# Order of VectorE's and ScalarE's work in the attention periods of a sigmoid-attention and MLP kernel

## The chip, the cores and the metric

The kernel runs on one core of one Trainium2 chip. The metric is the device time of one execution in microseconds (us); of several runs the median counts. Engines are named as in the profile: PE (TensorE) multiplies matrices and writes PSUM, PEld is its weight load, DVE is VectorE, ACT is ScalarE, POOL is GpSimd, SP is SyncE, on whose queue all DMAs are issued.

## What is computed

```python
scores = (q @ k.transpose(0, 1, 3, 2)) / sqrt(64) - log(448)     # 8 batches, 12 heads, 448 rows, 64 columns
attn   = sigmoid(scores)
x      = (attn @ v).transpose(0, 2, 1, 3).reshape(3584, 768)
out    = square(maximum(x @ w_in, 0)) @ w_out                      # 768 -> 2048 -> 768
```

`q`, `k`, `v` are 32-bit floats; `w_in` and `w_out` come as 64-bit floats, and the kernel makes 32-bit ones of them itself, from the two 32-bit words of each number.

## The kernel before

**The attention** works on pairs of heads: 48 pairs, two in each of 24 periods, numbered d = 0 to 23. `block(d)` (line 435) writes out by hand, for every engine, the order of the work of period d; nothing reorders it later. With n = 2d, TensorE computes in a period first `sr` (line 288), the rows left over of both pairs, then three score tiles of 128 rows for pair n and three for pair n+1 (`sc`, line 272), and then `pav`, the product with v, of pair n and of pair n+1 (lines 303 and 315). Score matmuls run in three passes on a split of x (here q and k of a pair): `high` (line 494, `qh`) casts x to a rounded part on VectorE, `low` (line 498, `ql`) subtracts that from x; the passes are high by high, high by low, low by high. ScalarE applies the sigmoid to each tile (`at` and `rest`, line 260).

Score tiles and `pav` share four PSUM tiles in rotation (`two`, line 537). A period takes nine of them, in the order `sr`, three `sc`, three `sc`, two `pav`; so the second score tile of a period takes the place of `pav` of pair n-2, and the third that of pair n-1. Each `pav` comes in two halves. `take(n)` (line 321) copies one half to SBUF on ScalarE, `put(n)` (line 325) adds the other half to it on VectorE: these are the *sums of x* (`xo`), the attention's output.

**The weights' words** are converted beside the attention. Chunks of 768 numbers a row (`f`) are loaded by `weights_load`, two operations of ScalarE treat the upper words (line 148) and the lower ones (line 149), and a *join* puts them together: three operations of VectorE (lines 153, 154, 157) and an integer add of GpSimd (line 160). Of two joined chunks VectorE makes four sums of blocks (lines 169 to 172), and chunk and sums are stored. `weights_of(piece, n)` spreads these steps over the pairs. In a period the *first* place for a join or for the four weight sums is ahead of `put(n-2)`, the *second* is ahead of the last `low`.

**The MLP** computes each product of 2x2 blocks by seven products of sums of blocks. The sums of x for its first group are *pieces* (`x_operands`, line 343): pieces 1, 2, 3, 6 split blocks of x into a high part (three casts on ScalarE, line 332) and a low part (three subtractions on VectorE, line 336, put off to the next period's list `later`); `t1`, `t2`, `t3` are three subtractions each (line 361) in place. `PIECES` and `T_PIECES` (lines 67 and 68) name the periods in which they are made. The MLP's weights are split in the same way by `halve_weights` (line 233): a cast on ScalarE (line 237) and a subtraction on VectorE (line 238). After the attention come, four times, a first product (`gemm1`, `ha`, `hb`, `hc`, line 547) and a second (`gemm2`, `oa`, `ob`, `oc`).

**SBUF tiles** come from pools of equal slots (`op2` with 35, `op1` with 20, `wide` with 8); a load whose slot isn't free waits on SP, and what is queued on SP behind it waits too. Before period 0, eight matmuls on zeros (line 765) keep TensorE at work while the first loads run.

Of the kernel before, what the change touches and what calls it, by code (L numbers as in the profile page):

```python
# [63 lines left out]
DEFERRED = (5, 6, 7)  # L64


PIECES = {12: (1,), 14: (2,), 20: (3,), 22: (6,)}
T_PIECES = {22: ("t1", "t2"), 23: ("t3",)}


@with_exitstack
def sigmoid_attention_relu2_mlp(
# [46 lines left out]
    nc = tc.nc  # L119
# [24 lines left out]

    def convert_words(t, w):
        nc.scalar.activation(w, t[:, :, 1], AF.Abs)
        nc.scalar.mul(out=t.bitcast(I32)[:, :, 0], in_=t.bitcast(U32)[:, :, 0], mul=2.0**-29)

    def convert_join(t, w):
# [29 lines left out]
    def deferred(i, at):  # L181


        f, a, s = {}, {}, {}

        def load(n, u, k):
            t = op2(f"fd{n}_{i}").rearrange("p a s -> p (a s)")[:, : 2 * HALF]
            nc.sync.dma_start(out=t.bitcast(I32), in_=w_out[u][:, k * HALF : (k + 1) * HALF].bitcast(I32))
            f[n] = t.rearrange("p (n w) -> p n w", w=2)

        def block(n):
            return op1(f"b{n}_{i}")[:, :HALF]

        def words(n):
            a[n] = block(n)
            convert_words(f[n], a[n])

        def add_up():
            for n in (5, 6, 7, 3):
                s[n] = block(n)  # L200
            nc.vector.tensor_add(out=s[5], in0=a[0], in1=a[4])
            nc.vector.tensor_sub(out=s[6], in0=s[5], in1=a[1])
            nc.vector.tensor_sub(out=s[7], in0=a[1], in1=a[0])
            nc.vector.tensor_sub(out=s[3], in0=a[2], in1=s[6])

        def store():
            for n, t in (a | s).items():
                if n:
                    nc.sync.dma_start(out=w2[i][:, PLACE[1][n]], in_=t)

        out = []
        for b, (n, u, k) in enumerate(((1, i, 0), (0, i, 1), (4, i + NI, 0), (2, i + NI, 1))):
            out.append((at + 3 * b - 5, lambda n=n, u=u, k=k: load(n, u, k)))
            out.append((at + 3 * b, lambda n=n: words(n)))
            out.append((at + 3 * b + 1, lambda n=n: convert_join(f[n], a[n])))
        out.append((at + 12, add_up))
        out.append((at + 13, store))
        return out
# [11 lines left out]
    def load_w1(i, parts, name):  # L230
        return load_weights([w1[i][:, part] for part in parts], name)

    def halve_weights(w):

        hi, lo = w
        raw = lo.bitcast(F32)
        nc.scalar.copy(out=hi, in_=raw)  # L237
        nc.vector.tensor_sub(out=lo, in0=raw, in1=hi.bitcast(F32))  # L238
        return w


# [159 lines left out]
    last = len(pairs) - 1  # L401
    todo = [(m, i) for m in range(2) for i in range(NI) if m == 0 or i not in DEFERRED]
    x, vt, xs, at, pav, xo, f64, w = {}, {}, {}, {}, {}, {}, {}, {}
    ready, stores, later = [], [], []
    pieces = {}
    ops = {}

    def half(j, h):
        return w[j].rearrange("p a n -> p (a n)")[:, (DM, 0)[h] : (2 * DM, DM)[h]]
# [9 lines left out]
    def weights_words(k):  # L419
        j, h = divmod(k, 3)  # L420
        if j < len(todo) and h < 2:
            if h == 0:
                w[j] = wide(f"a_{j}")
            convert_words(f64[j, h], half(j, h))

    def weights_join(k):
        j, h = divmod(k, 3)
# [7 lines left out]
    def block(d):  # L435


        n = 2 * d
        more = n + 2 <= last
        for m in (n + 4, n + 5):  # L440
            load(m)
        if more:
            vt[d + 1] = load_v(*divmod(d + 1, NP // 2))
        for store in ready:
            store()
        ready.clear()
        if d == 0:
            for m in (1, 2):
                high(m)
                low(m)  # L450
            score(0, (x[0],), ((0, 0),))
            rest = scores_rest(0, (x[0], x[1]))
        else:
            take(n - 1)
            weights_of(weights_join, n - 2)
            put(n - 2)
            high(n + 2)
            put(n - 1)
            low(n + 2)
            for piece in later:  # L460
                piece()
            later.clear()
            pieces_of(*T_PIECES.get(d, ()))
            rest = scores_rest(d, (x[n], x[n + 1]))
            score(n, xs[n])
        score(n + 1, xs[n + 1])
        for m in (n + 2, n + 3):
            weights_of(weights_load, m)
        high(n + 3)
        weights_of(weights_join, n - 1)  # L470
        low(n + 3)
        weights_of(weights_words, n)
        if more:
            for store in stores:
                store()
            stores.clear()
        for m in (n, n + 1):
            pav[m] = two(f"pav_{m}")
        attn_v(n, pav[n], at[n], vt[d])
        attn_v_rest((pav[n], pav[n + 1]), rest, vt[d])  # L480
        take(n)
        weights_of(weights_words, n + 1)
        attn_v(n + 1, pav[n + 1], at[n + 1], vt[d])
        for name in PIECES.get(d, ()):
            pieces[name](later)
# [17 lines left out]
    def take(n):  # L503
        xo[n] = take_x(*pairs[n], pav[n])
# [165 lines left out]
    def gemm2(g, blocks, operands1, weights1, ahead):  # L670
# [24 lines left out]
        def put(name, e, b, add):  # L695
            k, r = {"11": ("c", 0), "12": ("a", 0), "21": ("b", NE), "22": ("b", NE)}[name]
            o = op1(f"o{name}_{g}_{e}")
            to = outT[(r + e) * P : (r + e + 1) * P, (2 * g + b) * S : (2 * g + b + 1) * S]
            if add is not None:
                nc.vector.tensor_add(out=o, in0=banks[k, e], in1=snaps[add, e])  # L700
            elif g == NG - 1 and e == NE - 1:

                half = slice(S // 2), slice(S // 2, S)
                nc.scalar.copy(out=o[:, half[0]], in_=banks[k, e][:, half[0]])
                nc.vector.tensor_copy(out=o[:, half[1]], in_=banks[k, e][:, half[1]])
                for h in half:
                    nc.sync.dma_start(out=to[:, h], in_=o[:, h])
                return
            else:
                nc.scalar.copy(out=o, in_=banks[k, e])  # L710
            nc.sync.dma_start(out=to, in_=o)
# [47 lines left out]
    with tc.manual_schedule():  # L759
        with ExitStack() as attention:  # L760
            pools += [attention.enter_context(tc.tile_pool(name=f"two{i}", bufs=1, space=PSUM)) for i in range(3)]
            pools.append(ps1)
            wp = two("warm_ps")
            for i in range(8):
                nc.tensor.matmul(wp[:, 0], warm[:, :P], warm[:, :S], start=True, stop=True)
            load(0)
            load(1)
# [2 lines left out]
            load(3)  # L770
            for k in range(2):
                weights_load(k)
            for d in range(len(pairs) // 2 - 2):
                block(d)
                if d == KEPT * NP // 2:
                    ops[0], made = x_operands(0)
                    pieces.update(made)
            load_first(0, False)
            block(len(pairs) // 2 - 2)
            load_first(0, True)  # L780
            for i in (1, 2):
                load_first(i, False)
            halve_weights(first[0, False])
            block(len(pairs) // 2 - 1)
            halve_weights(first[1, False])
            take(last)
            put(last - 1)
            put(last)
        turn = itertools.count()
        pools = [ctx.enter_context(tc.tile_pool(name=f"bank{i}", bufs=2, space=PSUM)) for i in range(3)]  # L790
# [65 lines left out]
```

## Time and profile before

| | |
|---|---|
| runs | 1080.77, 1081.07, 1082.45 us; median 1081.07 |
| profiled execution | 1085.26 us, span of its instructions 1083.2 us |
| granted TensorE clock | 1.000 |
| busy in 16.33 to 258.28 us (periods 1 to 23) | PE 233.40, DVE 210.16, ACT 203.92, POOL 57.99 of 241.95 us |
| busy in 873 to 975.5 us (last first product) | PE 102.50, DVE 57.20, ACT 44.37 of 102.5 us |

A line of the timeline is: start, duration, engine, line of the kernel, operation, out<-in, partitions x elements, count, and in brackets the idle time of the engine ahead of it with what ended that. A line of the sums of a stretch is: the stretch, its length, and for PE, PEld, DVE, ACT and POOL the busy time with the number of instructions, then granted clock, DMA share and GB/s. A line of the waits is: who waited <- for whom: us in all, times, the longest. A line of page part 5 or 6 gives a group's count and mean; an issue's last number is the time until the data has landed. An engine that is off the path to the end can be idle without cost.

### The profile page before, as it was taken

To read this page: it belongs to the slowest core of one execution; us is meant where nothing else is said; L and a number is where in the kernel's file an instruction comes from. 1 tells how busy PE (TensorE), PEld (TensorE's weight loads), DVE (VectorE), ACT (ScalarE), POOL (GpSimd) and SP (SyncE) were. 2 spreads that over 40 slices of the span, in tenths; PEclk is the share of its full clock that TensorE was granted. 3 is DMA by queue.
4 is the path that set the end of the run, shared out by engine and by line. 5 is a ranking of instruction groups with operands and counts; after the bars stand their busy time and mean duration, and the time that the engine had idled before them with its cause. 6 is when DMAs were issued, how large, how long until landed. Compare 5 with 4: busy or idle time off the path is not lost.

```text
span 1083.2 us, 16127 instructions
## 1 busy us (share of the span) xinstructions
PE 1069.8 (99%) x6434; PEld 892.7 (82%) x6434; DVE 788.0 (73%) x889; ACT 634.0 (59%) x796; POOL 72.5 (7%) x42
## 2 busy tenths in 40 slices
PE   9999999999999999999999999999999999999998
PEld 4555545556999999999999999999999999999997
DVE  6997988996688898725579874456897825579931
ACT  7888879876676765534454654344565524455721
POOL 1222231310121000000000000000000000000000
PEclk9999999999999999999999999999999999999999
DMA  9979998880666435543342465333435533333441
GB/s 353 374 286 323 374 361 299 332 303 28 241 234 211 146 115 167 206 133 102 103 139 73 149 223 181 104 102 102 119 116 189 202 122 115 109 102 99 139 142 51
DMA packets 83451, 196.87 MB, mean 182 GB/s; under 512 B 6704, under 2 KB 57776, under 8 KB 83376
## 3 DMA queue, kind: packets, MB, share of 16 engines
q1 hardware_dynamic: 83376, 195.85, 52.3%
q8 instruction: 50, 0.82, 0.3%
q14 instruction: 25, 0.20, 0.1%
HBM read 154.53 MB, written 41.29 MB: 181 GB/s over the span
## 4 chain that ended last, share of the span: by engine, by line
PE 87%; DVE 7%; ACT 2%; issue 1%; DMA 1%; POOL 0%; SPq 0%; ACTq 0%; DVEq 0%
PE ha L547 22%; PE oa L547 22%; PE hb L547 11%; PE ob L547 11%; PE pav L303 5%; PE oc L547 5%; PE hc L547 5%; PE sc L272 5%; DVE qh L494 2%; DVE ql L498 1%; DVE xo L325 1%; DVE a L153 1%; PE pav L315 1%; ACT at L260 1%; PE sr L288 1%
## 5 line engine op out<-in xcount | busy, mean ns | idle before, releaser
L238 DVE TENSOR_TENSOR w_1l<-w_1l,w_1h 128x1536 fp32r<-128x1536 f32 x60 | 105.9, 1765 | 75.4 <-ACT w_1h L237 74.9
L590 ACT COPY s<-ha 128x448 f32<-128x448 f32 x96 | 51.0, 531 | 137.5 <-PE ha L547 124.1
L260 ACT ACTIVATE at<-sc 128x896 f32<-128x896 f32 x144 | 120.1, 937 | 9.2 <-PE sc L272 9.2
L303 PE MATMUL pav<-at,v 64*64 64x448 f32 x1152 | 118.1, 540 | 0.0
L237 ACT CAST w_1h<-w_1l 128x1536 fp32r<-128x1536 f32 x60 | 88.7, 1479 | 19.9 <-DMA w_1l<-w 19.6
L303 PEld LDWEIGHTS pav<-at,v 64*64 64x64 f32 x1152 | 41.6, 133 | 60.8 <-issue 52.8
L238 DVE TENSOR_TENSOR w_5l<-w_5l,w_5h 128x1152 fp32r<-128x1152 f32 x32 | 43.3, 1354 | 42.6 <-ACT w_5h L237 42.6
L237 ACT CAST w_0h<-w_0l 128x1536 fp32r<-128x1536 f32 x28 | 41.4, 1480 | 49.0 <-DMA w_0l<-w 49.0
L160 POOL TENSOR_TENSOR a<-a,f 128x768 int32<-128x768 int32 x26 | 58.0, 2230 | 168.4 <-DVE a L157 80.3
L238 DVE TENSOR_TENSOR w_0l<-w_0l,w_0h 128x1536 fp32r<-128x1536 f32 x28 | 49.2, 1756 | 20.7 <-ACT w_0h L237 20.5
L272 PE MATMUL sc<-qh 64*128 64x448 f32 x282 | 55.3, 388 | 8.6 <-DVE xo L325 8.6
L627 DVE TENSOR_TENSOR g<-hb,s 128x448 f32<-128x448 f32 x32 | 19.9, 622 | 45.9 <-PE hb L547 45.9
L272 PEld LDWEIGHTS sc<-qh 64*128 64x128 f32 x282 | 26.6, 184 | 31.0 <-PE pav L303 16.2
L272 PE MATMUL sc<-qh,ql 64*128 64x448 f32 x282 | 51.7, 362 | 0.1
L272 PE MATMUL sc<-ql,qh 64*128 64x448 f32 x282 | 51.7, 362 | 0.0
L494 DVE CAST qh<-x 128x896 fp32r<-128x896 f32 x47 | 46.1, 982 | 7.0 <-DMA x<-qk 7.0
L498 DVE TENSOR_TENSOR ql<-x,qh 128x896 fp32r<-128x896 f32 x47 | 50.9, 1082 | 0.1
L237 ACT CAST w_5h<-w_5l 128x1152 fp32r<-128x1152 f32 x32 | 37.1, 1159 | 22.3 <-DMA w_5l<-w 22.2
L573 DVE SCALAR_TENSOR_TENSOR g<-g 128x896 f32<-128x896 f32 x40 | 43.6, 1090 | 1.1
L321 ACT COPY xo<-pav 128x448 f32<-128x448 f32 x48 | 26.2, 547 | 28.7 <-PE pav L303 14.2
L715 ACT COPY t<-oa 128x448 f32<-128x448 f32 x36 | 19.1, 531 | 33.0 <-PE oa L547 32.8
L325 DVE TENSOR_TENSOR xo<-pav,xo 128x448 f32<-128x448 f32 x48 | 29.5, 617 | 12.0 <-ACT xo L321 11.8
(522 smaller groups left out, 3097.9 us busy)
## 6 DMA issues: line engine op xcount, KB each, us to landing
w_1l<-w SPq DMA_DIRECT2D x60, 768.0 KB, 4.4
w_0l<-w SPq DMA_DIRECT2D x28, 768.0 KB, 4.6
x<-qk SPq DMA_DIRECT2D x47, 448.0 KB, 6.6
f<-w_in SPq DMA_DIRECT2D x16, 768.0 KB, 8.8
w_5l<-w SPq DMA_DIRECT2D x32, 384.0 KB, 4.0
v<-v SPq DMA_DIRECT2D x24, 448.0 KB, 7.4
outT<-o SPq DMA_DIRECT2D x47, 224.0 KB, 2.3
w<-s SPq DMA_DIRECT2D x13, 768.0 KB, 8.5
```

Source lines behind the costliest of these rows:

```text
L160: nc.gpsimd.tensor_tensor(out=wb, in0=wb, in1=t.bitcast(I32)[:, :, 0], op=ALU.add)
L237: nc.scalar.copy(out=hi, in_=raw)
L238: nc.vector.tensor_sub(out=lo, in0=raw, in1=hi.bitcast(F32))
L260: nc.scalar.activation(at, sc, AF.Sigmoid, bias=NEG_LOG_S, scale=SCALE)
L272: nc.tensor.matmul(sc[:, j], x[kp][rows, 1, ks], x[qp][rows, 0], start=(n == 0), stop=(n == len(passes) - 1),)
L303: nc.tensor.matmul(sums[columns, h], vt[rows, n % 2 * NT + t, columns], at[t][rows, j], start=(t == 0 and (n % 2, h) != (1, 1)), stop=(t = ...
L325: nc.vector.tensor_add(out=x, in0=sums[:, 0], in1=x)
L494: nc.vector.tensor_copy(out=xs[n][0], in_=x[n])
L498: nc.vector.tensor_sub(out=xs[n][1], in0=x[n], in1=xs[n][0].bitcast(F32))
L547: nc.tensor.matmul(out, a[:, c], b, start=first and n == 0, stop=last and n == 2, skip_group_check=True)
L573: nc.vector.scalar_tensor_tensor(out=t, in0=t, scalar=0.0, in1=t, op0=ALU.max, op1=ALU.mult)
L590: nc.scalar.copy(out=s, in_=banks["a", i])
```

## The change

- `put(n-2)` and `put(n-1)` stand in a row behind the first place of a period. Both casts `high(n+2)` and `high(n+3)` come later, behind each other, ahead of the second place, and both `low` in a row behind it.
- Loads of x run one pair further ahead (`load(4)` ahead of period 0, then n+5 and n+6).
- The conversion of words is a list of single operations, of which one is issued ahead of `take(n)` and up to two behind it.
- Piece 1 goes from period 12, and piece 2 from 14, to period 21; `t1` from 22 to 20 and `t2` from 22 to 21. The first weight of the MLP is loaded ahead of period 20 and no longer of 22, is cast at the end of period 20 and no longer of 22, and its subtraction goes on the list `later`.
- `put(46)` goes ahead of the second MLP weight's split.
- Seven warm-up matmuls for eight. The last output tile is copied in two halves on ScalarE, and the second half's DMA is issued from ScalarE's queue; before, VectorE copied the second half, and both were issued from SP.

VectorE at the start of period 2 (`a_167` is the first weight, `s_410` its four sums, `xo_2` and `xo_3` the sums of x of pairs 2 and 3), before:

```order
L157 SCALAR_TENSOR_TENSOR a_167<-f_0_0_1_96,a_167 128x768
L325 TENSOR_TENSOR xo_2_307<-pav_289,xo_2_307 128x448
L494 CAST qh_337<-x_0_204 128x896
L325 TENSOR_TENSOR xo_3_330<-pav_290,xo_3_330 128x448
L498 TENSOR_TENSOR ql_338<-x_0_204,qh_337 128x896
L494 CAST qh_407<-x_1_206 128x896
L169 TENSOR_TENSOR s_410<-a_167 128x384
```

The same place now:

```order
L160 SCALAR_TENSOR_TENSOR a_168<-f_0_0_1_95,a_168 128x768
L327 TENSOR_TENSOR xo_2_309<-pav_290,xo_2_309 128x448
L327 TENSOR_TENSOR xo_3_331<-pav_291,xo_3_331 128x448
L503 CAST qh_404<-x_0_101 128x896
L503 CAST qh_407<-x_1_204 128x896
L172 TENSOR_TENSOR s_410<-a_168 128x384
```

The second sum of x has moved from behind the cast to ahead of it.

VectorE in period 21 (sums of x of pairs 40 and 41; `x_0l` and `y_0` are low parts of a piece, `w_0_0_1l` that of the first MLP weight), before:

```order
L325 TENSOR_TENSOR xo_5_2772<-pav_2727,xo_5_2772 128x448
L498 TENSOR_TENSOR ql_2780<-x_2_2636,qh_2779 128x896
L336 TENSOR_TENSOR x_0l<-xo_3_711,x_0h 128x448
L336 TENSOR_TENSOR x_0l<-xo_4_817,x_0h 128x448
L336 TENSOR_TENSOR y_0_2760<-xo_5_839,y_0_2760 128x448
L494 CAST qh_2848<-x_3_2638 128x896
L169 TENSOR_TENSOR s_2851<-a_2597 128x384
```

And now, from the end of period 20:

```order
L507 TENSOR_TENSOR ql_2701<-x_0_2363,qh_2700 128x896
L507 TENSOR_TENSOR ql_2704<-x_1_2491,qh_2703 128x896
L156 TENSOR_SCALAR a_2580<-a_2580 128x768
...
L327 TENSOR_TENSOR xo_5_2760<-pav_2715,xo_5_2760 128x448
L338 TENSOR_TENSOR x_0l<-xo_3_712,x_0h 128x448
...
L338 TENSOR_TENSOR w_0_0_1l<-w_0_0_1l,w_0_0_1h 128x1536
L363 TENSOR_TENSOR xo_3_712<-xo_3_712,xo_0_562 128x448
L363 TENSOR_TENSOR xo_4_817<-xo_4_817,xo_1_584 128x448
L363 TENSOR_TENSOR xo_5_840<-xo_5_840,xo_2_688 128x448
L503 CAST qh_2836<-x_2_2493 128x896
L503 CAST qh_2839<-x_3_2621 128x896
```

The weight's subtraction and `t2` have come between the piece and the casts; two `low` stand in a row ahead of the join that opens the period.

ScalarE at the end of period 20, from the last sigmoid to the `rest` of period 21, now:

```order
L262 ACTIVATE at_5_2_2698<-sc_5_2_2691 128x896
L152 ACTIVATE f_1_4_1_2440<-f_1_4_1_2440 128x768
L323 COPY xo_4_2733<-pav_2714 128x448
L334 CAST x_0h<-xo_3_712 128x448
L334 CAST x_0h<-xo_4_817 128x448
L334 CAST y_0_2749<-xo_5_840 128x448
L334 CAST w_0_0_1h<-w_0_0_1l 128x1536
L323 COPY xo_5_2760<-pav_2715 128x448
L262 ACTIVATE rest_2780<-sr_2775 128x896
```

The conversion and the weight's cast are new there; the three casts and both copies stood there before.

The diff, cut to its core:

```diff
@@ -64,8 +64,9 @@
 DEFERRED = (5, 6, 7)
 
 
-PIECES = {12: (1,), 14: (2,), 20: (3,), 22: (6,)}
-T_PIECES = {22: ("t1", "t2"), 23: ("t3",)}
+PIECES = {20: (3,), 21: (1, 2), 22: (6,)}
+T_PIECES = {20: ("t1",), 21: ("t2",), 23: ("t3",)}
+FIRST_W1 = 20
 
 
 @with_exitstack
@@ -144,8 +145,10 @@
 
 
 
-    def convert_words(t, w):
+    def convert_upper(t, w):
         nc.scalar.activation(w, t[:, :, 1], AF.Abs)
+
+    def convert_lower(t, w):
         nc.scalar.mul(out=t.bitcast(I32)[:, :, 0], in_=t.bitcast(U32)[:, :, 0], mul=2.0**-29)
 
     def convert_join(t, w):
@@ -193,7 +196,8 @@
 
         def words(n):
             a[n] = block(n)
-            convert_words(f[n], a[n])
+            convert_upper(f[n], a[n])
+            convert_lower(f[n], a[n])
 
         def add_up():
             for n in (5, 6, 7, 3):
@@ -230,12 +234,10 @@
     def load_w1(i, parts, name):
         return load_weights([w1[i][:, part] for part in parts], name)
 
-    def halve_weights(w):
+    def halve_weights(w, later=None):
 
         hi, lo = w
-        raw = lo.bitcast(F32)
-        nc.scalar.copy(out=hi, in_=raw)
-        nc.vector.tensor_sub(out=lo, in0=raw, in1=hi.bitcast(F32))
+        split_to(hi, lo, lo.bitcast(F32), later)
         return w
 
 
@@ -401,7 +403,7 @@
     last = len(pairs) - 1
     todo = [(m, i) for m in range(2) for i in range(NI) if m == 0 or i not in DEFERRED]
     x, vt, xs, at, pav, xo, f64, w = {}, {}, {}, {}, {}, {}, {}, {}
-    ready, stores, later = [], [], []
+    ready, stores, later, words = [], [], [], []
     pieces = {}
     ops = {}
 
@@ -421,7 +423,13 @@
         if j < len(todo) and h < 2:
             if h == 0:
                 w[j] = wide(f"a_{j}")
-            convert_words(f64[j, h], half(j, h))
+            for piece in (convert_upper, convert_lower):
+                words.append(lambda piece=piece: piece(f64[j, h], half(j, h)))
+
+    def convert(count):
+        for piece in words[:count]:
+            piece()
+        del words[:count]
 
     def weights_join(k):
         j, h = divmod(k, 3)
@@ -437,7 +445,7 @@
 
         n = 2 * d
         more = n + 2 <= last
-        for m in (n + 4, n + 5):
+        for m in (n + 5, n + 6):
             load(m)
         if more:
             vt[d + 1] = load_v(*divmod(d + 1, NP // 2))
@@ -445,18 +453,15 @@
             store()
         ready.clear()
         if d == 0:
-            for m in (1, 2):
-                high(m)
-                low(m)
+            high(1)
+            low(1)
             score(0, (x[0],), ((0, 0),))
             rest = scores_rest(0, (x[0], x[1]))
         else:
             take(n - 1)
             weights_of(weights_join, n - 2)
             put(n - 2)
-            high(n + 2)
             put(n - 1)
-            low(n + 2)
             for piece in later:
                 piece()
             later.clear()
@@ -466,10 +471,13 @@
         score(n + 1, xs[n + 1])
         for m in (n + 2, n + 3):
             weights_of(weights_load, m)
+        high(n + 2)
         high(n + 3)
         weights_of(weights_join, n - 1)
+        low(n + 2)
         low(n + 3)
-        weights_of(weights_words, n)
+        for m in (n, n + 1):
+            weights_of(weights_words, m)
         if more:
             for store in stores:
                 store()
@@ -478,8 +486,9 @@
             pav[m] = two(f"pav_{m}")
         attn_v(n, pav[n], at[n], vt[d])
         attn_v_rest((pav[n], pav[n + 1]), rest, vt[d])
+        convert(1)
         take(n)
-        weights_of(weights_words, n + 1)
+        convert(2)
         attn_v(n + 1, pav[n + 1], at[n + 1], vt[d])
         for name in PIECES.get(d, ()):
             pieces[name](later)
@@ -700,11 +709,9 @@
                 nc.vector.tensor_add(out=o, in0=banks[k, e], in1=snaps[add, e])
             elif g == NG - 1 and e == NE - 1:
 
-                half = slice(S // 2), slice(S // 2, S)
-                nc.scalar.copy(out=o[:, half[0]], in_=banks[k, e][:, half[0]])
-                nc.vector.tensor_copy(out=o[:, half[1]], in_=banks[k, e][:, half[1]])
-                for h in half:
-                    nc.sync.dma_start(out=to[:, h], in_=o[:, h])
+                for columns, queue in ((slice(0, S // 2), nc.sync), (slice(S // 2, S), nc.scalar)):
+                    nc.scalar.copy(out=o[:, columns], in_=banks[k, e][:, columns])
+                    queue.dma_start(out=to[:, columns], in_=o[:, columns])
                 return
             else:
                 nc.scalar.copy(out=o, in_=banks[k, e])
@@ -761,7 +768,7 @@
             pools += [attention.enter_context(tc.tile_pool(name=f"two{i}", bufs=1, space=PSUM)) for i in range(3)]
             pools.append(ps1)
             wp = two("warm_ps")
-            for i in range(8):
+            for i in range(7):
                 nc.tensor.matmul(wp[:, 0], warm[:, :P], warm[:, :S], start=True, stop=True)
             load(0)
             load(1)
@@ -770,21 +777,23 @@
             load(3)
             for k in range(2):
                 weights_load(k)
-            for d in range(len(pairs) // 2 - 2):
+            load(4)
+            for d in range(len(pairs) // 2):
+                if d == FIRST_W1:
+                    load_first(0, False)
+                if d == len(pairs) // 2 - 1:
+                    load_first(0, True)
+                    for i in (1, 2):
+                        load_first(i, False)
                 block(d)
                 if d == KEPT * NP // 2:
                     ops[0], made = x_operands(0)
                     pieces.update(made)
-            load_first(0, False)
-            block(len(pairs) // 2 - 2)
-            load_first(0, True)
-            for i in (1, 2):
-                load_first(i, False)
-            halve_weights(first[0, False])
-            block(len(pairs) // 2 - 1)
+                if d == FIRST_W1:
+                    halve_weights(first[0, False], later)
+            put(last - 1)
             halve_weights(first[1, False])
             take(last)
-            put(last - 1)
             put(last)
         turn = itertools.count()
         pools = [ctx.enter_context(tc.tile_pool(name=f"bank{i}", bufs=2, space=PSUM)) for i in range(3)]
```

## The prediction

> **What bounds the kernel now.** I read the page first, then the sums of two stretches, then the waits, then the timeline engine by engine. On the page TensorE has work nearly all the time:
>
> ```profile
> PE 1069.8 (99%) x6434; PEld 892.7 (82%) x6434; DVE 788.0 (73%) x889; ACT 634.0 (59%) x796; POOL 72.5 (7%) x42
> ```
>
> So only time in which PE stands still can be won. The sums for periods 1 to 23 of the attention, and the two largest PE entries that the waits view has inside it:
>
> ```profile
> 16.33:258.28 241.95, 233.40 (x2304) 128.99 (x2297) 210.16 (x285) 203.92 (x270) 57.99 (x26) 1.00 0.86 318
> ...
> PE sc L272 <- DVE xo L325: 8.6, 10, 2.0
> ```
>
> The 8.55 us in which PE is not busy there (241.95 - 233.40) is that wait: score matmuls wait for a sum of x on VectorE. The loss is larger than the idle time, because the drawn-out end of the matmul before a stall counts as busy. The loss is read from the starts of the periods instead (each starts with the first `sr` matmul; `ha` is the MLP's first):
>
> ```profile
> 26.34 0.93 PE L288 MATMUL sr<-x 64*64 64x448 f32 x8
> ...
> 29.15 0.47 PE L272 MATMUL sc<-qh 64*128 64x448 f32 x2 [0.48 <-DVE xo L325]
> ...
> 47.19 0.93 PE L288 MATMUL sr<-x 64*64 64x448 f32 x8
> ...
> 48.75 0.37 PE L272 MATMUL sc<-qh 64*128 64x448 f32 x2
> ...
> 49.36 0.36 PE L272 MATMUL sc<-qh 64*128 64x448 f32 x2
> ...
> 57.20 0.93 PE L288 MATMUL sr<-x 64*64 64x448 f32 x8
> ```
>
> Period 4 (47.19 to 57.20) runs without a stall in 10.01 us. 23 such periods are 230.23 us; the stretch takes 241.95, so **11.72 us** is lost, and that is all an attention without stalls could give back. The rows also give the deadlines inside a period: the second score tile starts 1.56 us behind the first `sr` (48.75 - 47.19) and the third 2.17 us. By the rotation of the four PSUM pools these two tiles take the banks of the two `pav` of the period before, so the sums of x of pairs n-2 and n-1 must have ended by +1.5 and +2.1 us.
>
> Why they are late, in period 2:
>
> ```profile
> 26.00 0.62 DVE L325 TENSOR_TENSOR xo<-pav,xo 128x448 f32<-128x448 f32 x1
> 26.53 2.03 DVE L494 CAST qh<-x 128x896 fp32r<-128x896 f32 x1
> 28.48 0.61 DVE L325 TENSOR_TENSOR xo<-pav,xo 128x448 f32<-128x448 f32 x1
> ...
> 30.02 0.61 DVE L494 CAST qh<-x 128x896 fp32r<-128x896 f32 x1
> ...
> 26.21 1.87 POOL L160 TENSOR_TENSOR a<-a,f 128x768 int32<-128x768 int32 x1 [2.14 <-DVE a L157]
> ...
> 26.58 0.53 ACT L321 COPY xo<-pav 128x448 f32<-128x448 f32 x1
> ```
>
> The cast behind the first sum takes 2.03 us where the next one takes 0.61: it starts while GpSimd's add (the join's last step) runs and ends 0.48 us after that add (28.56 against 28.08). The second sum's other input was there at 27.11 (26.58 + 0.53), but it stands behind the cast and ends at 29.09; PE goes on at 29.15. The sum at 26.00 is not slowed by the add.
>
> **The change part by part.** *Sums in a row.* Both sums now stand ahead of the casts. The second can end 0.77 + 0.62 = +1.4 us into the period (input at 27.11 - 26.34 = +0.77), 0.7 ahead of its deadline, provided that what stands ahead of the first sum ends by about +0.9. That is the first join or the four weight sums, and their start hangs on VectorE's queue in the period before:
>
> ```profile
> 40.13 0.55 DVE L153 TENSOR_SCALAR a<-a 128x768 f32<-128x768 f32 x1
> ...
> 42.19 1.08 DVE L498 TENSOR_TENSOR ql<-x,qh 128x896 fp32r<-128x896 f32 x1
> 45.03 0.56 DVE L169 TENSOR_TENSOR s<-a 128x384 f32<-128x384 f32 x1 [1.75 <-POOL a L160]
> ...
> 47.04 0.61 DVE L325 TENSOR_TENSOR xo<-pav,xo 128x448 f32<-128x448 f32 x1
> ...
> 42.40 2.59 POOL L160 TENSOR_TENSOR a<-a,f 128x768 int32<-128x768 int32 x1 [4.74 <-ACT at L260]
> ...
> 282.88 2.34 DVE L238 TENSOR_TENSOR w_1l<-w_1l,w_1h 128x1536 fp32r<-128x1536 f32 x1
> ...
> 282.57 1.04 POOL L160 TENSOR_TENSOR b<-b,fd 128x384 int32<-128x384 int32 x1 [55.71 <-DVE b L157]
> ...
> 247.18 1.76 DVE L238 TENSOR_TENSOR w_1l<-w_1l,w_1h 128x1536 fp32r<-128x1536 f32 x1 [3.99 <-ACT w_1h L237]
> ```
>
> From start to start a join takes 2.06 us (40.13 to 42.19) and four weight sums 2.01 (45.03 to 47.04). A subtraction that starts ahead of the add stretches the add to 2.59 us; one that starts behind it waits (2.34 against 1.76) and ends about 1.6 of its 1.76 us behind the add's end. So of two `low` in a row behind the second join, which the change makes, the first runs free and the second waits: it ends 42.40 + 2.59 + 0.94 - 40.13 = 5.8 us after that join's start, where two free ones would end after 4.1. No row shows that pair; the nearest row is this one, and I take the full 1.7 us. A clean period with joins in both places then runs: sums to +1.4, casts to +2.5, second join +2.5 to +4.6, second `low` to +8.3, weight sums of the next period to +10.3 = +0.3, first sum to +0.9. Deadline +1.5: kept by 0.6. For a first join whose lower words are the last that ScalarE converts:
>
> ```profile
> 43.76 1.00 ACT L148 ACTIVATE a<-f 128x768 f32<-128x768 f32 x1
> ```
>
> The first conversion behind the sigmoids ends at 44.76, 2.4 us ahead of the next period (47.19); a join behind it has ended by that period's start. Kept as well. So periods 1 to 19 lose their stalls.
>
> *Words as single operations* takes one conversion from ahead of the copy `take(n)` and puts it behind. PE's deadlines see ScalarE's conversions only through the sums of x, which have the 0.7 us above, so I cost it at nothing; without that cover it is one conversion, up to 1.0 us, in a period. *Loads of x one pair earlier* and *one warm-up matmul less* cost nothing either: PE's chain at the start hangs on x_1's load and the two operations behind it, not on the warm-ups:
>
> ```profile
> 1.15 3.17 PE L765 MATMUL warm_ps<-warm 128*128 128x448 bf16 x8 [1.15 <-DVE warm L399]
> ...
> 9.20 0.47 PE L272 MATMUL sc<-qh,ql 64*128 64x448 f32 x2
> ...
> 7.39 0.63 DVE L494 CAST qh<-x 128x896 fp32r<-128x896 f32 x1 [6.29 <-DMA x<-qk]
> 8.05 1.09 DVE L498 TENSOR_TENSOR ql<-x,qh 128x896 fp32r<-128x896 f32 x1
> ```
>
> Without that cover a warm-up is worth 3.17 / 8 = 0.4 us.
>
> *MLP pieces in periods 20 to 23.* These add VectorE work where joins still stand:
>
> ```profile
> 238.23 3.29 DVE L361 TENSOR_TENSOR xo<-xo,xo 128x448 f32<-128x448 f32 x6
> ...
> 245.21 0.56 ACT L332 CAST yt<-xo 128x448 fp32r<-128x448 f32 x1
> 245.68 1.47 ACT L237 CAST w_1h<-w_1l 128x1536 fp32r<-128x1536 f32 x1
> 247.05 0.53 ACT L321 COPY xo<-pav 128x448 f32<-128x448 f32 x1
> ...
> 249.62 0.47 PE L272 MATMUL sc<-qh 64*128 64x448 f32 x2 [2.00 <-DVE xo L325]
> ```
>
> PE now stands idle for 2.00 us in period 23, because the weight's cast and subtraction (1.47 and 1.76) stand ahead of its sums; that goes. A subtraction of a piece is 3.29 / 6 = 0.54 us, two casts are 1.1. Period 20: sums to +1.4, three subtractions (t1) to +3.0, casts to +4.1, join and `low` pair (5.8) to +9.8, the next join to +11.9, the first sum to +12.45, that is +2.44 of period 21, where +1.5 is wanted: **0.94 lost**. Period 21 from +2.9, behind its second sum: three subtractions of piece 3 (1.6, the first waiting 0.9 for the join's add), the weight's (1.7), t2's three (1.6), casts 1.1, weight sums 2.0, two `low` 2.0, together 10.9. So the first sum of period 22 runs from +13.75 to +14.37; that period starts at 10.01 + 0.94 = 10.95, which makes it +3.42 against 1.5: **1.92 lost**. ScalarE's additions (three casts at 0.47 from start to start and the weight's 1.47 in period 20, six casts, 2.8 us, in 21) stand ahead of a copy whose sum VectorE reaches later still, and are covered by that. Period 22 holds 7.4 us of VectorE work (sums 1.1, six subtractions 3.2, casts 1.1, `low` 2.0), period 23 less; they lose nothing.
>
> *The last output tile.*
>
> ```profile
> 1079.73 0.35 ACT L704 COPY o<-oa 128x224 f32<-128x224 f32 x1 [4.42 <-PE oa L547]
> 1080.11 0.39 DVE L705 COPY o<-oa 128x224 f32<-128x224 f32 x1 [14.63 <-ACT o L704]
> ...
> 1080.10 0.81 SPq L707 DMA_DIRECT2D outT<-o  x2
> ```
>
> The two halves run one after the other now too, on two engines; on one engine the second ends about 0.1 us earlier. An issue from ScalarE's queue is in no row; by SP's rows (0.81 / 2) the second issue saves or adds up to 0.4. I take -0.1. [...]
>
> **The sum.** Lost now 11.72; left 0.94 + 1.92, and I leave 0.2 for small waits; gain 8.66, with the end's 0.1 8.8. The profiled execution took 1085.26 us (span 1083.2) and would come to 1076.5. It is 4.2 above the median of the runs, and the excess lies in its last stage:
>
> ```profile
> 419.07 14.59 PE oa L547 x72
> ...
> 1064.81 14.89 PE oa L547 x72
> ```
>
> That 2% over the last 210 us is 4.2; it does not touch the attention, so the gain is taken from the median: 1081.07 - 8.8 = **1072.3**.
>
> [...] If the pair were not held up, joins and sums of periods 21 and 22 would be 1.7 us earlier, and the time 1071.
>
> **The rivals.** (1) The adds last longer than here, since VectorE now offers work at once: a GpSimd add of 3.6 us instead of 2.59 moves the first sum from +0.9 past its deadline by 0.3 in the 12 periods that follow a second join, 3.6 us: 1076. For it speaks that the add stretches (1.87 to 2.59); against it that the sums of x ran beside it at 0.62. Chance 0.14. (2) Periods 21 and 22 lose next to nothing, because VectorE runs ahead further than my queue says: 1081.07 - 11.7 = 1069.4. Chance 0.09. (3) PE's stalls have another cause than the sums' place and stay: 1081. Against it: PE starts 0.06 us behind the second sum's end (29.15, 29.09). Chance 0.03. (4) Slower: the first MLP weight, now loaded at period 20, comes late. Its cast stands on ScalarE ahead of `take(41)`, the `rest` and all sigmoids of period 21, so each us of lateness is one of PE.
>
> ```profile
> f<-w_in SPq DMA_DIRECT2D x16, 768.0 KB, 8.8
> ...
> SPq L226 <- DVE w_1l L238: 9.4, 1, 9.4
> ```
>
> Its load waits on SP for a buffer that GpSimd's add of period 19 frees at +7.4 at the latest (second join to +4.6, add 2.8), with two loads of x behind it; with 8.8 us to land it is there at +6.2 of period 20. Its cast stands behind three others that follow the copy for pair 40, and is due at about +9.8. Slower than before needs 3.6 + 8.8 = 12.4 us more, more than the longest such wait on SP (9.4): 1083 if it takes 14. Chance 0.04. My forecast has 0.70.
>
> The range takes in the forecast with -2.3 (pair not held up, a first join on time) and reaches to rival 1: 1070.0 to 1076.0. A measurement of this kernel tells about 0.2%, 2.2 us, from no change; forecast, rivals 1 and 2 are faster by more: 0.93; rival 3 same, 0.03; rival 4 slower, 0.04.
>
> **What would show it.** Right: periods 1 to 20 of 10.0 us; no cast of 2.0 us between two sums of x; a `low` of about 2.7 us behind each second join; stalls of 0.9 and 1.9 us in periods 21 and 22 and none in 23. Wrong: periods above 10.1 us spread over the attention (rival 1), ScalarE waiting for a DMA in period 20 (rival 4), or a period 22 without a stall (rival 2).

## The result, and the profile after

| | before | now |
|---|---|---|
| median of six runs each | 1081.83 us | 1073.27 us |
| lowest and highest | 1080.77, 1093.98 us | 1071.84, 1075.73 us |
| profiled execution, its span | 1085.26, 1083.2 us | 1073.47, 1071.7 us |
| granted TensorE clock of that execution | 1.000 | 0.998 |

The ratio of the means is 0.9899, 95% interval 0.9855 to 0.9944; one run of before, at 1093.98, draws it down. By the medians the change is 8.6 us faster where 8.8 was forecast. Single runs of several kernels lie 3 us or more above the rest at an undiminished clock, 1075.73 here; where single runs are compared below, these are left out and the others are called undisturbed.

The page's row of engines, then the three largest entries of TensorE in the waits, now:

```profile
PE 1064.9 (99%) x6433; PEld 894.4 (83%) x6433; DVE 789.1 (74%) x888; ACT 636.3 (59%) x797; POOL 72.5 (7%) x42
```

```profile
PE sc L274 <- DVE xo L327: 1.6, 2, 0.9
PE warm_ps L772 <- DVE warm L401: 1.2, 1, 1.2
PE sc L274 <- DVE ql L507: 0.5, 1, 0.5
```

The waits for a sum of x have fallen from 8.6 us in ten places to 1.6 us in two. The stretch of periods 1 to 23 (from the first `sr` of period 1 to the MLP's first `ha`):

```profile
15.86:250.61 234.75, 232.65 (x2305) 130.84 (x2297) 213.04 (x287) 206.56 (x271) 58.08 (x26) 0.99 0.88 328
```

It takes 234.75 us where it took 241.95; 4.52 us above 23 clean periods (230.23) are left of 11.72.

Period 2 on VectorE, the place whose rows carried the argument:

```profile
26.07 1.24 DVE L327 TENSOR_TENSOR xo<-pav,xo 128x448 f32<-128x448 f32 x2
27.22 1.96 DVE L503 CAST qh<-x 128x896 fp32r<-128x896 f32 x2
...
41.35 2.75 DVE L507 TENSOR_TENSOR ql<-x,qh 128x896 fp32r<-128x896 f32 x1
```

Both sums are one row of 1.24 us and end at 27.31, 1.45 us into the period (25.86); they ended at +2.75 before. The casts, not the sums, now meet GpSimd's add: the two take 1.96 us beside it (it runs from 26.28 to 28.15 us), 1.15 in the next period. The third row is the second `low` behind a second join, in period 3: 2.75 us, where the first of such a pair takes about 1.1.

TensorE in periods 2 and 21 to 23:

```profile
25.86 0.93 PE L290 MATMUL sr<-x 64*64 64x448 f32 x8
...
35.87 0.93 PE L290 MATMUL sr<-x 64*64 64x448 f32 x8
...
215.99 0.93 PE L290 MATMUL sr<-x 64*64 64x448 f32 x8
...
218.46 0.47 PE L274 MATMUL sc<-qh 64*128 64x448 f32 x2 [0.75 <-DVE xo L327]
...
227.00 0.93 PE L290 MATMUL sr<-x 64*64 64x448 f32 x8
...
228.82 0.47 PE L274 MATMUL sc<-qh,ql 64*128 64x448 f32 x2 [0.49 <-DVE ql L507]
...
230.36 0.47 PE L274 MATMUL sc<-qh 64*128 64x448 f32 x2 [0.86 <-DVE xo L327]
...
231.63 0.58 PE L274 MATMUL sc<-ql,qh 64*128 64x448 f32 x2
232.00 0.58 PE L274 MATMUL sc<-qh 64*128 64x448 f32 x2
...
240.48 0.93 PE L290 MATMUL sr<-x 64*64 64x448 f32 x8
250.61 0.47 PE L556 MATMUL ha<-x_0h,w_1h 128*128 128x448 f32 x1
```

Period 2 takes 10.01 us, as does every period up to 20. Period 21 takes 11.01 (1.00 lost; 0.94 forecast). Period 22 takes 13.48, so 3.47 are lost, where 1.92 was forecast. The two waits in its rows account for about the forecast part (1.8 us); the rest is in the rows at 231.63 and 232.00, which start 0.37 us apart where such rows start 0.20 apart elsewhere. The sums of that stretch show why:

```profile
230.00:235.00 5.00, 4.64 (x30) 4.08 (x30) 5.00 (x10) 3.72 (x5) 0.00 (x0) 0.66 0.86 271
```

The granted clock is 0.66 of full speed over these 5 us: 0.34 x 5 = 1.7 us lost, or 3.4 us at half speed; from 231.63 to 234.24 us it is 0.50. In the six runs of the new kernel the mean clock is 0.998 in three (1073.07, 1073.47, 1073.70 us) and 1.000 in the others (1071.84, 1071.94 and 1075.73); 1.7 us lost in 1071.7 are just those 0.002. So there are two questions left: what carries the gain, and what that half clock belongs to.

### The profile page after: what moved, and what is told of

Same layout as the page of the kernel before. It is cut to its first block, busy times and chain, and to the rows that moved or that the text cites. A ratio compares the mean times of both kernels' runs of the same rounds, so it can differ in the third digit from the quotient of the medians.

```text
span 1071.7 us, 16172 instructions
## 1 busy us (share of the span) xinstructions
PE 1064.9 (99%) x6433; PEld 894.4 (83%) x6433; DVE 789.1 (74%) x888; ACT 636.3 (59%) x797; POOL 72.5 (7%) x42
## 4 chain that ended last, share of the span: by engine, by line
PE 97%; DVE 2%; issue 0%; ACT 0%
PE ha L556 22%; PE oa L556 22%; PE ob L556 11%; PE hb L556 11%; PE pav L305 10%; PE sc L274 8%; PE hc L556 5%; PE oc L556 5%; PE pav L317 2%; PE sr L290 1%; DVE ql L507 1%; DVE xo L363 0%; PE warm_ps L772 0%; DVE xo L327 0%; DVE qh L503 0%; DVE x_0l L338 0%
## 5 line engine op out<-in xcount | busy, mean ns | idle before, releaser
L507 DVE TENSOR_TENSOR ql<-x,qh 128x896 fp32r<-128x896 f32 x47 | 72.4, 1581 | 0.0
L503 DVE CAST qh<-x 128x896 fp32r<-128x896 f32 x47 | 31.3, 705 | 7.0 <-DMA x<-qk 7.0
```

The costliest lines, as they stand in the source:

```text
L503: nc.vector.tensor_copy(out=xs[n][0], in_=x[n])
L507: nc.vector.tensor_sub(out=xs[n][1], in0=x[n], in1=xs[n][0].bitcast(F32))
```

## The experiments

Theory T is that of the prediction: the stalls up to period 20 go by the place of the sums of x alone; what is left in periods 21 and 22 is VectorE's MLP work put there; and, added to it now, the half clock follows from the stalls of period 22. Rivals: the gain comes from ScalarE's words (A) or from the pieces' new periods (B); the half clock comes by chance (C); others stand with their runs.

### The cast between the sums again

```diff
             put(n - 2)
+            high(n + 2)
             put(n - 1)
...
-        high(n + 2)
+        if d == 0:
+            high(n + 2)
         high(n + 3)
```

> The changed kernel with one thing put back: the first cast (qh of pair n+2) stands between the two sums of x again, in periods 1 to 22; all else stays. Theory T (the stalls came from a cast between the sums that GpSimd's add holds up): by the row durations added in VectorE's order the attention loses about 7.4 us for the 2.9 that the changed kernel's order gives, so about 4.5 us slower than the changed kernel, near 1077.5, with the loss in stalls of 0.7 to 0.9 us in the periods that follow a join in both places (2, 5, 10, 13, 18) and in period 21. Rival A (the gain came from ScalarE's single word operations): no change from the changed kernel, 1073. Rival B (it came from moving pieces 1 and 2 out of periods 12 and 14): no change either, 1073.

Measured: 1077.2 us (before on this chip 1082.43; ratio 0.9952, 0.9929 to 0.9975). VectorE in period 2, and TensorE's entry in the waits:

```profile
25.71 0.62 DVE L327 TENSOR_TENSOR xo<-pav,xo 128x448 f32<-128x448 f32 x1
26.24 2.02 DVE L505 CAST qh<-x 128x896 fp32r<-128x896 f32 x1
28.18 0.61 DVE L327 TENSOR_TENSOR xo<-pav,xo 128x448 f32<-128x448 f32 x1
```

```profile
PE sc L274 <- DVE xo L327: 4.3, 7, 1.6
```

The cast of 2.02 us is back between the sums, and so are the stalls: periods 2, 5, 10, 13 and 18, the ones that the expectation lists, lose 0.7 to 0.85 us each. Neither words nor pieces were touched, so neither rival can give this. Period 21 (220.08 to 234.09) loses 4.0 us: 1.7 at half clock again (granted clock 0.83 from 220 to 230 us), and 2.3 in stalls.

### Words in twos again

```diff
-        for m in (n, n + 1):
-            weights_of(weights_words, m)
+        weights_of(weights_words, n)
...
-        convert(1)
+        convert(2)
         take(n)
+        weights_of(weights_words, n + 1)
         convert(2)
```

> The changed kernel with ScalarE's word operations in twos as before: both operations of pair n ahead of the copy take(n), both of pair n+1 behind it. Theory T (the sums' place alone took the stalls away; the single word operations are worth nothing): within 0.5 us of the changed kernel, 1073.3, periods 1 to 20 of 10.0 us. Rival A (the single operations took the stalls away, by bringing the copies of take earlier): most of the 8.5 us comes back, 1079 to 1082, with score matmuls that wait for sums whose copy on ScalarE came late.

Measured: 1073.89 us (0.9926, 0.9896 to 0.9957); its five undisturbed runs at clock 1.000 stand at 1071.81 to 1072.13, as the changed kernel's two at 1071.84 and 1071.94. Periods 3 to 20 take 10.0 us; periods 1 and 2 lose 0.26 and 0.06, which was not expected. Rival A has fallen: the single operations are worth nothing here.

### The sums alone

To the kernel before only this was done:

```diff
             put(n - 2)
-            high(n + 2)
             put(n - 1)
+            high(n + 2)
             low(n + 2)
```

> The kernel before with one thing changed: the second sum of x stands directly behind the first one, ahead of the first cast and its low part. Theory T: of the 11.3 us that the row durations added in VectorE's order give for before, 5.0 are left, so 6.3 us faster than before, near 1075.5; what stays is about 2 us in period 23 (the first MLP weight's split ahead of its sums) and 0.6 to 1.0 us in periods 13, 15 and 17 (the pieces). Rival A (ScalarE's words) and rival B (the pieces' place): within 1 us of before, 1081 to 1082, and stalls in every third period as before.

Measured: 1075.01 us, 7.4 us faster than before's median (0.9922, 0.9896 to 0.9948); between the undisturbed runs at clock 0.999 or 1.000 (1074.37 to 1075.08 against 1080.32 to 1081.30, the middle ones 1074.9 and 1080.65) it is 5.7. TensorE's entry in the waits, and its row in period 23:

```profile
PE sc L272 <- DVE xo L325: 3.4, 4, 2.0
```

```profile
243.33 0.47 PE L272 MATMUL sc<-qh 64*128 64x448 f32 x2 [2.00 <-DVE xo L325]
```

Moving one line gives some 6 of the 9 us. In the profile the attention loses 5.4 us (251.98 - 16.34, less 230.23) for the 5.0 of the expectation and the 11.72 of before, most of it where the theory left it: 2.4 us in period 23 behind the weight's split, 0.6 to 1.0 in 13, 15 and 17. Rival B as the whole cause has fallen too.

### The pieces as before

```diff
-PIECES = {20: (3,), 21: (1, 2), 22: (6,)}
-T_PIECES = {20: ("t1",), 21: ("t2",), 23: ("t3",)}
-FIRST_W1 = 20
+PIECES = {12: (1,), 14: (2,), 20: (3,), 22: (6,)}
+T_PIECES = {22: ("t1", "t2"), 23: ("t3",)}
+FIRST_W1 = 22
...
-                    halve_weights(first[0, False], later)
+                    halve_weights(first[0, False])
```

> The changed kernel with the MLP's pieces as before: pieces 1 and 2 in periods 12 and 14, t1 and t2 in 22, the first weight loaded at 22 and split at the end of 22, its subtraction directly behind the cast. Theory T (moving the pieces only moved the loss, from 13, 17 and 23 to 21 and 22): by the row durations added in VectorE's order the attention loses 3.1 us (0.6 in period 13, 0.4 in 17, 2.1 in 23) for the 2.9 of the changed kernel, so within 0.7 us of the changed kernel's runs at full clock, 1072.2. Rival B (the pieces' move carries the gain): several us slower than the changed kernel, 1076 or more.

Measured: 1074.23 us (0.9925, 0.9908 to 0.9941), 2 us more than expected. TensorE's entry in the waits and the sums of two stretches in period 23 (236.62 to 250.57):

```profile
PE sc L274 <- DVE xo L327: 2.3, 2, 2.0
```

```profile
235.00:240.00 5.00, 3.35 (x34) 1.25 (x26) 2.09 (x2) 4.94 (x8) 0.00 (x0) 1.00 0.19 79
240.00:245.00 5.00, 4.65 (x30) 4.52 (x30) 3.94 (x8) 3.11 (x4) 0.00 (x0) 0.66 0.00 0
```

The stalls are where they were expected: 0.63 in period 13, 0.38 in 17 and, without the half clock, some 2.2 in 23; with 0.1 in period 20 that is 3.3 for the changed kernel's 2.9. The surplus is a stretch at half clock behind the 2.00 us stall (0.66 of full speed again, 1.7 us), and all six runs show a mean clock of 0.998. By stalls alone the move of the pieces gains only 0.4 us: it shifts the loss from periods 13, 17 and 23 into 21 and 22. The other 1.7 us are the clock.

The sums alone left 5.4 us where this kernel's stalls leave 3.3, with the pieces in the same periods. The 2.1 us between them lie mostly in periods 14, 15, 17 and 20. So they come from what else the change does: casts and low parts further back, loads one pair earlier, the order at the end. No run takes these apart; the single word operations are out by the run with words in twos.

### t1, t2 and the weight one or two periods later

```diff
-T_PIECES = {20: ("t1",), 21: ("t2",), 23: ("t3",)}
+T_PIECES = {21: ("t1",), 22: ("t2",), 23: ("t3",)}
...
-                if d == FIRST_W1:
+                if d == FIRST_W1 + 2:
                     halve_weights(first[0, False], later)
```

> The changed kernel with t1 in period 21 and t2 in 22 (changed kernel: 20 and 21), and the first MLP weight's split at the end of period 22 for 20. Theory T (what is left in periods 21 and 22 is VectorE's work for the MLP put there, and the half clock for 3.4 us follows from the stalls of period 22): excess of the attention 0.7 us for 2.9, and no half clock, so 2.2 us faster than the changed kernel's runs at full clock and 3.7 faster than those at half: 1069.6, clock 1.000 in every run. Rival C (the half clock comes by chance, whatever PE does): clock 0.998 in about half of the runs still, and a median near 1070.5. Rival D (the stalls of periods 21 and 22 have another cause, GpSimd's adds or ScalarE's casts, which are still there): 1072 to 1073, unchanged.

Measured: 1069.49 us (0.9879, 0.9840 to 0.9917), the fastest kernel of this study. Its stretch of periods 1 to 23:

```profile
15.42:246.40 230.98, 230.84 (x2304) 129.69 (x2297) 213.03 (x287) 205.94 (x271) 58.07 (x26) 1.00 0.89 333
```

230.98 us is 0.75 above 23 clean periods (forecast 0.7), in periods 22 and 23. No wait of TensorE for a sum of x is left in the waits, and none of the six runs shows 0.998. Rival D has fallen as far as GpSimd's adds and the pieces' casts go, which are still there. The weight's cast on ScalarE moved too, together with its subtraction; for this one the rows of the changed kernel in period 21 decide:

```profile
217.15 0.53 ACT L323 COPY xo<-pav 128x448 f32<-128x448 f32 x1
...
216.91 0.96 DVE L160 SCALAR_TENSOR_TENSOR a<-f,a 128x768 int32<-128x768 int32 x1
217.79 1.15 DVE L327 TENSOR_TENSOR xo<-pav,xo 128x448 f32<-128x448 f32 x2
```

The copy behind that cast has ended at 217.68, ahead of the join on VectorE (217.87), so the sums waited for VectorE. Rival C, that the clock falls by chance, has six runs against it, which is little: at the 8 in 30 of the kernels that keep the changed kernel's stalls (last section), six without one come in about one case of six.

### A longer stall

```diff
         high(n + 3)
+        for _ in range(3 if d == 21 else 0):
+            nc.vector.tensor_copy(out=xs[n + 3][0], in_=x[n + 3])
```

> The changed kernel with three more casts of x of pair 45 in period 21 (into the same tile, the same values), ahead of the second place: 3 x 0.5 us of VectorE ahead of the first sum of period 22. Theory T (the stalls of period 22 bring the half clock, the more surely the longer they are): the stalls of period 22 grow by 1.6 us to 3.5, and the half clock for 3.4 us is there in every run or nearly (granted clock 0.998), so 1.6 us slower than the changed kernel's runs at half clock: about 1075.2, no run below 1074. Rival C (the half clock comes by chance, whatever PE does): also 1.6 slower, but clock 1.000 in about half of the runs, with times of 1073.5 and 1075.2.

Measured: 1076.76 us (0.9962, 0.9940 to 0.9984), no run below 1075.72. TensorE's largest entry in the waits, and the sums of two stretches in period 22 (226.50 to 242.88):

```profile
PE sc L274 <- DVE ql L509: 2.5, 1, 2.5
```

```profile
230.00:235.00 5.00, 4.14 (x22) 3.16 (x24) 5.00 (x10) 2.35 (x3) 0.00 (x0) 0.55 0.86 298
235.00:240.00 5.00, 5.00 (x44) 3.06 (x44) 3.59 (x5) 3.16 (x4) 0.00 (x0) 0.77 0.98 368
```

All twelve runs show a mean clock of 0.998 or less, eight of them 0.996. In the profiled one (0.45 + 0.23) x 5 = 3.4 us are lost to the clock, 6.8 us at half speed: twice the stretch of the changed kernel. That is the part that the expectation lacked; period 22 loses 6.37 us, of which 3.4 is clock and 3.0 stall (3.5 expected). So the half clock belongs to the stalls of the period: with the longer stall it comes in twelve runs of twelve, and lasts twice as long in most of them. That it comes the more surely the longer the stall is holds for these kernels alone (last section).

### A join between the two low parts

```diff
-        weights_of(weights_join, n - 1)
         low(n + 2)
+        weights_of(weights_join, n - 1)
         low(n + 3)
```

> The changed kernel with one low part (ql of pair n+2) ahead of the second place for joins and the other behind it, for both behind it. Both start ahead of GpSimd's add, so none should be held up: 1.1 us each for 1.1 and 2.7. Theory T: VectorE's queue is 1.7 us shorter behind a second join, but what follows in the next period (the weight sums, or a join whose words ScalarE converts last) waits for the add or for ScalarE anyway, so the stalls of periods 21 and 22 stay (1.0 and 1.9) and the time is that of the changed kernel within 0.3 us. Rival G (the held-up low is what delays the sums of periods 21 and 22): period 21 loses nothing and 22 about 1 us less, 1.5 to 2 us faster than the changed kernel, and no run at half clock.

Measured: 1072.24 us (0.9911, 0.9892 to 0.9930). VectorE and GpSimd at the end of period 20, and TensorE in period 21:

```profile
212.12 1.08 DVE L507 TENSOR_TENSOR ql<-x,qh 128x896 fp32r<-128x896 f32 x1
213.12 2.21 DVE L156 TENSOR_SCALAR a<-a 128x768 f32<-128x768 f32 x1
...
212.33 2.58 POOL L163 TENSOR_TENSOR a<-a,f 128x768 int32<-128x768 int32 x1 [9.05 <-DMA x<-qk]
...
217.51 0.47 PE L274 MATMUL sc<-qh 64*128 64x448 f32 x2 [0.77 <-DVE xo L327]
```

The page's group of low parts, first in the changed kernel, then here:

```profile
L507 DVE TENSOR_TENSOR ql<-x,qh 128x896 fp32r<-128x896 f32 x47 | 72.4, 1581 | 0.0
```

```profile
L507 DVE TENSOR_TENSOR ql<-x,qh 128x896 fp32r<-128x896 f32 x47 | 50.7, 1082 | 0.0
```

The 47 low parts now take 1082 ns on average for 1581, but where a join opens the next period its first operation takes 2.21 us for 0.55: it runs into the same add (212.33 + 2.58 = 214.91) and ends 0.42 us behind it. Period 21 (from 215.02) loses 1.03, as in the changed kernel 1.00. The time behind the add is not saved; the next operation in the row spends it. Rival G has fallen.

### Start and end as before

```diff
-            for i in range(7):
+            for i in range(8):
```

and the last output tile as in the kernel before.

> The changed kernel with eight warm-up matmuls for seven and the last output tile as before (second half copied by VectorE, both halves issued from SP's queue). Theory T (neither is on the path): within 0.3 us of the changed kernel; 3.5 us from the start of the last ScalarE copy to the end of the span; period 1 starts when x_1's load lets it, between 15.3 and 16.3 us as in the other runs. Rival E (the warm-up stands on TensorE's path): 0.4 us slower, period 1 at 16.3 in place of 15.3 to 16.0, and the first score tile 0.4 later. Rival F (the second issuing queue saves an issue): the stretch behind the last copy 0.1 to 0.4 longer than 3.50.

Measured: 1072.47 us (0.9908, 0.9891 to 0.9926). Its five runs at clock 1.000 stand at 1072.25 to 1072.51; on the same chip the four undisturbed ones of the last experiment, with seven warm-ups and the same stalls, stand at 1071.51 to 1072.49, with the middle at 1071.94, 0.5 less. TensorE at the start, here and then in the last experiment:

```profile
1.15 3.17 PE L774 MATMUL warm_ps<-warm 128*128 128x448 bf16 x8 [1.15 <-DVE warm L401]
4.25 3.79 PE L274 MATMUL sc<-x 64*128 64x448 f32 x12
7.98 0.98 PE L290 MATMUL sr<-x 64*64 64x448 f32 x8
...
16.23 0.93 PE L290 MATMUL sr<-x 64*64 64x448 f32 x8
```

```profile
3.88 2.73 PE L274 MATMUL sc<-x 64*128 64x448 f32 x12
6.54 0.98 PE L290 MATMUL sr<-x 64*64 64x448 f32 x8
```

There is no gap between the warm-ups, the first scores and `sr`, so the eighth moves the first score from 3.88 to 4.25. It reaches period 1 where nothing waits between: from `sr` to period 1 it is 8.25 us here (7.98 to 16.23) and in three other profiles, 8.34 to 8.67 in the rest, where x_1's split is late. Period 1 starts at 16.23 to 16.34 us in the three profiles with eight warm-ups and at 14.88 to 16.05 in the seven with seven. So rival E is right that the warm-up stands on TensorE's chain, but 0.4 us is the most that it costs. Where the stretch from `sr` to period 1 is longer than 8.25 us, TensorE waits there, and the wait takes up part of a later start. An estimate from the seven profiles with seven warm-ups, 0.37 us less the wait of each, gives 0 to 0.37, 0.2 on average. The 0.5 by the times is a difference of two ranges that overlap, and the starts of period 1 don't measure it either: the twelve first scores take from 2.73 to 3.99 us in the ten profiles, at a granted clock that reads 1.00 in the six of them in which the first 5 or 10 us were read, and why is not known. The end doesn't show rival F. The rows of the changed kernel:

```profile
1068.16 0.59 ACT L713 COPY o<-oa 128x224 f32<-128x224 f32 x2 [4.33 <-PE oa L556]
1068.54 0.33 SPq L714 DMA_DIRECT2D outT<-o  x1
1068.79 0.37 ACTq L714 DMA_DIRECT2D outT<-o  x1
```

From the first copy to the end of the span it is 3.5 us (1071.7 - 1068.16), and 3.5 with the old tile (1070.4 - 1066.93), though the second issue starts 0.25 us behind the first. The warm-up and the tail were changed in one kernel; the rows at the two ends tell them apart, the times alone would not.

## Why the prediction was right, and where it failed

- *Sums in a row.* Right: periods 1 to 20 take 10.0 us, the sums end at +1.45 (+1.4 forecast), and undoing or doing this step alone moves the time by 4 to 6 us. *Words* at nothing: right. *Loads of x* at nothing: no run tests it alone.
- *The second low part.* Right in its size, 2.75 us (2.7 forecast). The sentence that without this hold the time would be 1071 is wrong: it took it that the queue behind would come 1.7 us earlier, and the run with a join between the low parts shows the add holding that join's first operation in its place (2.21 us for 0.55).
- *Pieces in periods 20 to 23.* Right, and by the queue that the prediction wrote out: from the first subtraction of period 21 to the first sum of period 22 VectorE takes 10.84 us (218.85 to 229.69) for the 10.9 of the sum. Lost are 1.00 and, in the profile of the last experiment, which has no half clock, 1.88 us (period 22 from 227.37 to 239.26), for 0.94 and 1.92. With the 0.1 of period 23 that run's attention loses 2.91 us; the sum had 3.06.
- *One warm-up at nothing.* Wrong. The step said that TensorE's chain at the start hangs on x_1's load; that holds for the one execution whose rows it read, where the cast of x_1 starts at 7.39. In the nine other profiles it starts at 5.94 to 6.97, and in four of them the chain runs through the warm-ups without a gap. The 0.4 us that the step named for a lost cover is the most that a warm-up costs by the rows, 0.2 the estimate on average.
- *The last tile at -0.1.* Nothing came of it.
- *Left out:* the half clock, 1.5 us in three of the six runs (1073.47 against 1071.94). The errors in warm-up and clock work against each other. That the median lies within 1 us of the forecast is luck in part: it depends on how many of the six runs have the half clock. Without it the new kernel stands at 1071.9, 0.4 below the forecast.
- *The rivals.* GpSimd's adds lasted 2.58 us at most (rival 1: 3.6); the stalls up to period 20 are gone (rival 3), those of 21 and 22 are there (rival 2); the first MLP weight was there when ScalarE came to it (rival 4):

```profile
215.31 0.56 ACT L334 CAST y<-xo 128x448 fp32r<-128x448 f32 x1
215.78 1.47 ACT L334 CAST w_1h<-w_1l 128x1536 fp32r<-128x1536 f32 x1
```

- *The profiled executions.* Before's excess of 4.2 us lay in its last stage, as said; it isn't in the new one, so 11.8 us between the two profiles is no measure of the change. Of it 7.67 lie ahead of the first `ha` (258.28 - 250.61).

## What to carry to other kernels

Read the deadline of a buffer from the consumer's rows and put what frees it ahead of what runs longer beside another engine; here that was a cast of 2.03 us for 0.61 beside GpSimd's add, and moving one line gave two thirds of the gain. A stall cost more here than its idle time where the clock fell behind it: taking away 2.2 us of stalls (2.91 to 0.75) moved the runs at full clock by 2.6 us (their middle from 1071.89 to 1069.25), and the median by 3.8 (1073.27 to 1069.49), since no run is left at half clock. And one profile of the start, where the cast of x_1 waits for its load and starts between 5.94 and 7.39 us in the ten profiles, is one sample of which chain is the longer.

## What the runs showed of the hardware

- *Half clock behind short stalls.* Two waits of 0.49 and 0.86 us in one period, 1.9 us lost, were followed in some runs by 3.4 us at half the full clock; in the profile of the changed kernel the granted clock was 0.50 from 231.63 to 234.24 us. Runs at 0.998 or below: none of 6 where a period loses at most 0.45 us, 8 of 30 over four kernels with the 1.9 of period 22, 6 of 6, 3 of 9 and 13 of 43 with a wait of 2.0 us in period 23 (pieces as before, sums alone, the kernel before), 6 of 12 with the 2.3 of the cast between the sums, 12 of 12 with 3.0. Only the profiled runs show where the clock fell. By the sums of their stretches it was 3.4 us at half clock behind the stalls of the changed kernel's period 22 and behind the 2.00 us wait of the run with the pieces as before (0.66 over 5 us in both), and 6.8 behind the longer stall (0.55 and 0.77 over 5 us each); the longest wait of TensorE in these profiles is 2.5 us. What decides, at equal stalls, between a run with and one without it stays open. The length of the wait alone doesn't: on one chip and with the same wait of 2.00 us, the kernel before shows it in 2 of 17 runs and the one with the pieces as before in 6 of 6.
- *A one-input operation of VectorE took longer beside GpSimd's add too.* A TENSOR_SCALAR took 2.21 us for 0.55 beside it, as the cast of the prediction took 2.03 for 0.61; they ended 0.42 and 0.48 us behind the add. The sums of x, with one input in PSUM, stayed at 0.62.
